# Attention with keys on partitions and transposed channel mixing, in a fused attention and MLP-mixer kernel

## The chip, the cores and the metric

The kernel runs on one core of a Trainium2 chip. The metric is the time of one execution on the device, in microseconds (us). The profile is that of one execution; its span runs from the first to the last instruction.

## What is computed

All numbers are float32, except that the four weights come as float64 words, which the kernel converts. Eight batch elements, 12 heads, 448 tokens, head size 64. The output of attention, heads side by side, goes through a mixer that first mixes tokens and then channels.

```
rmsnorm(x, g) = x / sqrt(mean(x*x) + 1e-6) * g           # over the head size
scores = (rmsnorm(q, g_q) @ rmsnorm(k, g_k).T) / 8
attn   = exp(scores - max(scores)); attn /= sum(attn) + 1e-9
x      = (attn @ v), heads beside one another            # (8, 448, 768)
u      = x + (relu(x.T @ w_tok1) @ w_tok2).T             # 448 -> 256 -> 448
out    = u + relu(u @ w_ch1) @ w_ch2                     # 768 -> 1536 -> 768
```

## The kernel before

Tokens are cut into four chunks of 112 (token 4p + c is row p of chunk c). Attention goes by pairs of heads (48 pairs, six to a batch element) and, within a pair, by four steps, one for each chunk of queries; a step does both heads, called a = 0 and 1.

Before its steps a pair's q and k are loaded (`load_pair`, on SyncE's queue), squared on GpSimd (L208), summed on VectorE (L209), raised to the power -0.5 on GpSimd (L213) and scaled there into `qs` (L218). `trans_qk` transposes them on TensorE (L231), so that the two heads' 64 features lie on 128 partitions, and VectorE copies them out with the gains (L234).

A step's `score` (L247) has the queries stationary and the keys moving. The two heads use the upper and the lower 64 rows of the TensorE array. Scores come out with queries on partitions, 112 x 448, so the row maximum is a reduction on VectorE (L252), and the exponential on ScalarE (L254) takes it as its bias and sums each row on the way. A step later `trans_e` turns the exponentials round in four transposes for each head (L265), which VectorE and ScalarE copy out (L268, L270). Another step later `av` multiplies them with the values, eight products of 64 moving columns (L279). `finish_pair` divides by the sums and writes x with tokens on partitions (L295).

The mixer of one batch element is cut in small pieces. `tok1` (L330) and `tok2` (L340) mix tokens, L343 adds to x; `trans_u` (L350) turns u round, channels on partitions; `ch1` (L365) gives 12 blocks of 128 hidden channels; `ch2` (L380) takes h2 stationary and w_ch2 moving in 384 columns, L385 adds u, and each chunk of 112 tokens is stored.

Weights come in 80 chunks of at most 256 columns. A chunk's words are loaded on ScalarE's queue and converted by five operations on VectorE (L166, L167, L172, L174, L176), two on GpSimd (L169, L170) and one on ScalarE (L171). The first 44 chunks hold the token weights and w_ch1, the last 36 w_ch2.

`merge` interleaves two lists of pieces in proportion to their costs. The attention of batch element b is merged with the mixer of b - 1, that of 0 with the first 44 weight chunks; the last 36 are merged into the first part of the first mixer. The merged order is a priority; within it a scheduler may let an engine's ready instruction go ahead, TensorE's too. The eight PSUM banks are split: three for scores, two for all transposes of attention, one for its output, two for the mixer.

Of the kernel before, what the change touches and what calls it, by code (L numbers as in the profile page):

```python
# [8 lines left out]
F32 = mybir.dt.float32  # L9
U32 = mybir.dt.uint32  # L10
I64 = mybir.dt.int64
# [5 lines left out]

def merge(*lists):
    """Lists of (cost, function), each in its order, interleaved in proportion to their costs."""
# [16 lines left out]
def kernel(  # L36
    ctx: ExitStack,
    tc: tile.TileContext,
    q: bass.AP,
    k: bass.AP,  # L40
    v: bass.AP,
    g_q: bass.AP,
    g_k: bass.AP,
    moe_w_tok1: bass.AP,
    moe_w_tok2: bass.AP,
    moe_w_ch1: bass.AP,
    moe_w_ch2: bass.AP,
    out: bass.AP,
):
    nc = tc.nc  # L50

# [6 lines left out]
    R = S // NS  # tokens of a chunk; token NS * p + c is row p of chunk c  # L58
# [6 lines left out]
    assert S % NS == 0 and R <= P and 2 * D == P and H % 2 == 0  # L65
# [7 lines left out]
    qk_pool = pool("qk_pool", 3)  # L73
    v_pool = pool("v_pool", 4)
    sq_pool = pool("sq_pool", 1)
    qs_pool = pool("qs_pool", 2)
    st_pool = pool("st_pool", 4)
    qkT_pool = pool("qkT_pool", 2)
    e_pool = pool("e_pool", 3)
    eT_pool = pool("eT_pool", 2)  # L80
    x_pool = pool("x_pool", 2)
    ho_pool = pool("ho_pool", 3)
    uT_pool = pool("uT_pool", 1)
# [8 lines left out]
    one_c = const.tile([P, 1], F32, name="one_c")  # L92
# [14 lines left out]
    st = {}  # L107

# [4 lines left out]
    def weight_chunks():  # L113
        """(rows, source, destination, chunks that the destination splits the columns into, or None)."""
# [36 lines left out]
    def weight_convert(i):  # L151
        """Float64 words to the nearest float32: |w| = (1 + high / 2^20 + low / 2^52) * 2^e."""
# [15 lines left out]
        # Exponents past float32's become those of 0 and of infinity.  # L168
        nc.gpsimd.tensor_scalar(ef, e, 1151.0 * 2**20, 896.0 * 2**20, ALU.min, ALU.max)  # L169
        nc.gpsimd.tensor_scalar(e, ef, -896.0 * 2**20, 8.0, ALU.add, ALU.mult)  # L170
        nc.scalar.activation(out=mf, in_=m, func=AF.Identity, bias=one_c[0:rows], scale=2.0**-20)  # L171
# [16 lines left out]

    def load_pair(p):
        b, j = divmod(p, NPAIR)  # L190
        hs = slice(2 * j, 2 * j + 2)
# [4 lines left out]
        vt = v_pool.tile([P, 2, NS * D], F32, name="vt")  # L196
        nc.sync.dma_start(out=vt[0:R], in_=v[b, hs].rearrange("h (p c) d -> p h (c d)", c=NS))
        st["qk", p], st["v", p] = qk, vt

    def norm_pair(p):  # L200
# [4 lines left out]
        for i in range(2):  # L205
            x = qk[0:R, i].rearrange("p h x -> p (h x)")
            sq = sq_pool.tile([P, n * D], F32, name="sq")
            nc.gpsimd.tensor_tensor(out=sq[0:R], in0=x, in1=x, op=ALU.mult)  # L208
            nc.vector.tensor_reduce(  # L209
                out=ms[0:R, i * n:(i + 1) * n], in_=sq[0:R].rearrange("p (n d) -> p n d", d=D),  # L210
# [4 lines left out]
        for i in range(2):  # L215
            qs = qs_pool.tile([P, NS, 2, D], F32, name="qs")
            r = rs[0:R, i * n:(i + 1) * n].rearrange("p (h c) -> p h c", h=2)
            nc.gpsimd.tensor_tensor(  # L218
                out=qs[0:R].rearrange("p c h d -> p h c d"),
                in0=qk[0:R, i].rearrange("p h (c d) -> p h c d", d=D),  # L220
                in1=r.unsqueeze(3).to_broadcast([R, 2, NS, D]), op=ALU.mult)
            st["qs", p, i] = qs
        st.pop(("qk", p))

    def trans_qk(p, i):
# [3 lines left out]
        ps = ps_T.tile([P, 512], F32, name="t_ps", tag="T")  # L229
        for c in range(NS):  # L230
# [3 lines left out]
        nc.vector.tensor_scalar(  # L234
            st["qkT", p][:, i, :], ps[:, 0:S], g_t[:, i:i + 1], None, ALU.mult)

    def score(s):
        p, c = divmod(s, NS)
        qkT = st["qkT", p]
        if c == 0:  # L240
            st["den", p] = st_pool.tile([P, NS, 2], F32, name="den")
        e = e_pool.tile([P, 2, S], F32, name="e")
        nmax = st_pool.tile([P, 2], F32, name="nmax")
        pss = []
        for a in range(2):
            ps = ps_S.tile([P, 512], F32, name="s_ps")
            nc.tensor.matmul(  # L247
                out=ps[0:R, 0:S], lhsT=qkT[a * D:(a + 1) * D, 0, c * R:(c + 1) * R],
                rhs=qkT[a * D:(a + 1) * D, 1, :], start=True, stop=True)
            pss.append(ps)  # L250
        for a in range(2):
            nc.vector.tensor_reduce(  # L252
                out=nmax[0:R, a:a + 1], in_=pss[a][0:R, 0:S], axis=AX_X, op=ALU.max, negate=True)
            nc.scalar.activation(  # L254
                out=e[0:R, a, :], in_=pss[a][0:R, 0:S], func=AF.Exp, bias=nmax[0:R, a:a + 1],
                scale=1.0, accum_out=st["den", p][0:R, c, a:a + 1])
        st["e", s] = e

    def trans_e(s, a):
        e = st["e", s]  # L260
        if a == 0:
            st["eT", s] = eT_pool.tile([P, 2, S], F32, name="eT")
        ps = ps_T.tile([P, 512], F32, name="t_ps", tag="T")
        for kc in range(NS):
            nc.tensor.transpose(  # L265
                ps[0:R, kc * R:(kc + 1) * R], e[0:R, a, kc * R:(kc + 1) * R], ident[0:R, 0:R])
        if a == 0:
# [194 lines left out]
```

## Time and profile before

| | us |
|---|---|
| median of 3 runs | 1982.87 |
| lowest and highest run | 1979.45, 1983.07 |
| span of the profiled execution | 1979.2 |
| median less that span | 3.7 |
| mixer groups of a batch element begin at (L330) | 467.64, 696.57, 925.25, 1154.04, 1383.09, 1611.70, 1833.97 |

The profile gives no time of its execution other than the span. Engines are TensorE (PE; PEld is its loading of the stationary operand), VectorE (DVE), ScalarE (ACT), GpSimd (POOL) and SyncE (SP). A row of the table of groups gives line, engine, operation, output and inputs, shapes and count, then the busy time in us and the mean of one in ns, then the engine's idle time just before and what ended it. A TensorE record's end is modelled, so the cost of one in a dense stretch is read from the start of one group to the start of the next. A float32 product stands there as two records, a transpose as one.

### The profile page before, as it was taken

What the parts mean: (1) busy time and instruction counts of PE and PEld (TensorE: products, weight loads), DVE (VectorE), ACT (ScalarE), POOL (GpSimd) and SP (SyncE); (2) the same over time, 40 slices, a digit from 0 to 9 for tenths busy, and PEclk for the clock granted to TensorE, in tenths of its full rate; (3) what the DMA queues carried; (4) which work ended last, traced back from release to release, by engine and by line L of the source; (5) the groups of instructions that cost most, each with busy time, mean ns of one, the idle gap of its engine ahead of it and who ended that gap; (6) DMA issues with size and microseconds to landing.
All of it is one profiled execution on the core that took longest, in us unless ns stands there. A gap on an engine that the chain in (4) does not pass through costs nothing.

```text
span 1979.2 us, 22557 instructions
## 1 busy us (share of the span) xinstructions
PE 1904.1 (96%) x9152; PEld 1176.1 (59%) x9152; DVE 732.9 (37%) x1513; ACT 477.9 (24%) x1193; POOL 427.9 (22%) x408
## 2 busy tenths in 40 slices
PE   5888888999999999999999999999999999999999
PEld 3556554666656665666656666666666666566554
DVE  5677777233323332332422343233322333222100
ACT  2333333212221222222222122212222122221100
POOL 4444566112211211211121121122112111000000
PEclk9776988999999999999999999999999999999999
DMA  4222232011000100010000110011000100000000
GB/s 118 76 79 86 79 97 78 15 35 31 15 19 22 38 26 14 24 33 28 23 17 25 29 31 19 15 36 36 15 23 16 33 28 15 5 8 14 8 0 28
DMA packets 50535, 66.20 MB, mean 33 GB/s; under 512 B 4416, under 2 KB 36928, under 8 KB 50432
## 3 DMA queue, kind: packets, MB, share of 16 engines
q1 hardware_dynamic: 38656, 44.05, 7.6%
q10 hardware_dynamic: 11776, 20.72, 3.7%
q8 instruction: 72, 1.18, 0.3%
q14 instruction: 31, 0.25, 0.0%
HBM read 53.74 MB, written 11.01 MB: 33 GB/s over the span
## 4 chain that ended last, share of the span: by engine, by line
PE 87%; POOL 5%; DVE 5%; DMA 1%; issue 1%; ACT 0%; ACTq 0%; POOLq 0%; DVEq 0%
PE m_ps L380 26%; PE m_ps L365 21%; PE o_ps L279 14%; PE s_ps L247 9%; PE t_ps L265 7%; PE m_ps L330 4%; PE m_ps L340 3%; PE t_ps L231 2%; POOL rs L213 2%; POOL qs L218 1%; PE m_ps L350 1%; POOL e_t L170 1%; POOL e_t L169 1%; DVE nmax L252 1%; DMA qk<-in_q_dram 1%
## 5 line engine op out<-in xcount | busy, mean ns | idle before, releaser
L380 PE MATMUL m_ps<-wc_sb,h 128*112 128x384 f32 x1536 | 535.2, 491 | 0.0
L365 PE MATMUL m_ps<-uT,wc_sb 128*128 128x448 f32 x1152 | 477.8, 552 | 0.1
L279 PEld LDWEIGHTS o_ps<-vt,eT 112*112 112x112 f32 x3072 | 367.2, 189 | 133.4 <-issue 64.0
L279 PE MATMUL o_ps<-vt,eT 112*112 112x64 f32 x3072 | 369.9, 272 | 15.7 <-DVE eT L268 15.4
L380 PEld LDWEIGHTS m_ps<-wc_sb,h 128*112 128x112 f32 x1536 | 256.1, 177 | 198.0 <-issue 31.6
L254 ACT ACTIVATE e<-s_ps,nmax 112x448 f32<-112x448 f32 x384 | 240.3, 630 | 498.6 <-DVE nmax L252 497.0
L252 DVE TENSOR_REDUCE nmax<-s_ps 112x1 f32<-112x448 f32 x384 | 224.5, 619 | 271.0 <-PE s_ps L247 271.0
L218 POOL TENSOR_TENSOR qs<-qk,rs 112x512 f32<-112x512 f32 x96 | 99.3, 1050 | 999.3 <-PE t_ps L231 998.2
L365 PEld LDWEIGHTS m_ps<-uT,wc_sb 128*128 128x128 f32 x1152 | 205.9, 191 | 182.9 <-issue 180.8
L270 ACT COPY eT<-t_ps 112x448 f32<-112x448 f32 x192 | 102.0, 531 | 595.5 <-PE t_ps L265 585.0
L268 DVE COPY eT<-t_ps 112x448 f32<-112x448 f32 x192 | 119.2, 621 | 338.8 <-PE t_ps L265 179.1
L247 PE MATMUL s_ps<-qkT 64*112 64x448 f32 x768 | 226.1, 614 | 9.2 <-ACT e L254 5.7
L265 PE MATMUL t_ps<-ident,e 112*112 112x112 f32 x1536 | 198.6, 270 | 2.6 <-DVE eT L268 2.6
L265 PEld LDWEIGHTS t_ps<-ident,e 112*112 112x112 f32 x1536 | 169.1, 143 | 52.1 <-issue 33.3
L213 POOL TENSOR_TENSOR rs<-ms,mhalf_c 112x16 f32<-112x16 f32 x48 | 142.4, 2967 | 37.6 <-DVE ms L212 36.6
L208 POOL TENSOR_TENSOR sq<-qk 112x512 f32<-112x512 f32 x96 | 106.5, 1109 | 160.0 <-DMA qk<-in_q_dram 109.1
L247 PEld LDWEIGHTS s_ps<-qkT 64*112 64x112 f32 x768 | 61.7, 180 | 99.0 <-issue 49.1
L385 DVE TENSOR_TENSOR ob<-x,m_ps 112x384 f32<-112x384 f32 x64 | 35.3, 552 | 218.9 <-PE m_ps L380 218.9
L209 DVE TENSOR_REDUCE ms<-sq 112x8 f32<-112x512 f32 x96 | 65.6, 683 | 110.7 <-POOL sq L208 110.7
L340 PE MATMUL m_ps<-h,w_sb 128*112 128x384 f32 x256 | 93.4, 494 | 3.4 <-DVE x L343 3.4
L330 PE MATMUL m_ps<-x,w_sb 112*128 112x384 f32 x256 | 92.4, 505 | 3.9 <-DVE x L295 3.9
L234 DVE TENSOR_SCALAR qkT<-t_ps,g_t 128x448 f32<-128x448 f32 x96 | 63.0, 680 | 85.1 <-PE t_ps L231 85.0
(35 smaller groups left out, 787.1 us busy)
## 6 DMA issues: line engine op xcount, KB each, us to landing
raw<-in_moe_w_ch_dram ACTq DMA_DIRECT2D x72, 256.0 KB, 2.7
qk<-in_q_dram SPq DMA_DIRECT2D x48, 224.0 KB, 3.0
qk<-in_k_dram SPq DMA_DIRECT2D x48, 224.0 KB, 3.2
vt<-in_v_dram SPq DMA_DIRECT2D x48, 224.0 KB, 2.6
out_dram<-ob SPq DMA_DIRECT2D x32, 336.0 KB, 2.7
raw<-in_moe_w_tok_dram ACTq DMA_DIRECT2D x4, 224.0 KB, 5.0
raw<-in_moe_w_tok_dram ACTq DMA_DIRECT2D x2, 256.0 KB, 3.4
raw<-in_moe_w_tok_dram ACTq DMA_DIRECT2D x2, 192.0 KB, 2.4
```

Source lines behind the costliest of these rows:

```text
L213: nc.gpsimd.tensor_tensor(out=rs[0:R], in0=ms[0:R], in1=mhalf_c[0:R].to_broadcast([R, 2 * n]), op=ALU.pow)
L218: nc.gpsimd.tensor_tensor(out=qs[0:R].rearrange("p c h d -> p h c d"), in0=qk[0:R, i].rearrange("p h (c d) -> p h c d", d=D), in1=r.unsque ...
L247: nc.tensor.matmul(out=ps[0:R, 0:S], lhsT=qkT[a * D:(a + 1) * D, 0, c * R:(c + 1) * R], rhs=qkT[a * D:(a + 1) * D, 1, :], start=True, stop ...
L252: nc.vector.tensor_reduce(out=nmax[0:R, a:a + 1], in_=pss[a][0:R, 0:S], axis=AX_X, op=ALU.max, negate=True)
L254: nc.scalar.activation(out=e[0:R, a, :], in_=pss[a][0:R, 0:S], func=AF.Exp, bias=nmax[0:R, a:a + 1], scale=1.0, accum_out=st["den", p][0:R ...
L265: nc.tensor.transpose(ps[0:R, kc * R:(kc + 1) * R], e[0:R, a, kc * R:(kc + 1) * R], ident[0:R, 0:R])
L268: nc.vector.tensor_copy(out=st["eT", s][0:R, a, :], in_=ps[0:R, 0:S])
L279: nc.tensor.matmul(out=o[0:R, c, a, :], lhsT=eT[0:R, a, kc * R:(kc + 1) * R], rhs=vt[0:R, a, kc * D:(kc + 1) * D], start=(kc == 0), stop=( ...
L330: nc.tensor.matmul(out=ps[:, 0:HC], lhsT=w1_sb[0:R, c, jc * P:(jc + 1) * P], rhs=x[0:R, c, cs], start=(c == 0), stop=(c == NS - 1))
L340: nc.tensor.matmul(out=ps[0:R, 0:HC], lhsT=w2_sb[:, jc, c, :], rhs=st["h1", jc][:, cs], start=(jc == 0), stop=(jc == NJ - 1))
L365: nc.tensor.matmul(out=ps[:, 0:S], lhsT=wc1_sb[:, cc, f * P:(f + 1) * P], rhs=st["uT"][:, cc, :], start=(cc == 0), stop=(cc == NC - 1))
L380: nc.tensor.matmul(out=ps[0:R, 0:HC], lhsT=st["h2"][:, f, c * R:(c + 1) * R], rhs=wc2_sb[:, f, cs], start=(f == 0), stop=(f == NF - 1))
```

## The change

**Scores** come out with keys on partitions: `score` has the keys stationary and the queries moving (L251), one half of a pair (two chunks of keys, both heads) at a time. The exponential (L256) has no bias and no sum. There is no row maximum: a gate at the start computes the largest (g_q g_k)^2, and an `If` runs this arm where the scores cannot pass 60 in size; another arm of the same length, with the row maximum, stands behind it.

**Values** are stationary: `av` (L305) multiplies 64 value columns with 448 moving exponentials, the two heads in the left and the right 64 columns of the array, four products for each half pair, straight into channels on partitions. No transposes of e are left.

**Sums** of the exponentials over the key chunks are taken on VectorE in three additions of 112 x 896 (L291, L295), and over partitions by a product with ones (L319); a reciprocal (L328) and a product (L329) follow. The result is uT, channels on partitions.

**Mixing** keeps that form. `trans_x` (L375) makes x for `tok1`; `tok2` (L398) adds to uT; `ch1` (L413) is as before; `ch2` (L425) has w_ch2 stationary and h2 moving, 448 columns; `trans_y` (L437) turns the result round, and two stores of half a batch element each follow (L444).

**Order and space.** TensorE runs in the order in which the code is written; the other engines are still scheduled. Attention of the first two batch elements, and one pair more, goes ahead with the first 44 weight chunks; then the mixer of b is merged with the attention of b + 2, and the last two mixers run alone. q and k have two buffers instead of three, the squares lie in the buffers of `qs`; x and y share one buffer. Four banks hold scores, two the output of attention, two everything else.

```diff
+    ctx.enter_context(tc.manual_schedule(engines={nc.tensor.engine}))
...
-    qk_pool = pool("qk_pool", 3)
+    qk_pool = pool("qk_pool", 2)
...
+    uT_pool = pool("uT_pool", 3)
+    x_pool = pool("x_pool", 1)
...
-    ps_S = pool("ps_S", 3, space=PSUM)
-    ps_T = pool("ps_T", 2, space=PSUM)
-    ps_O = pool("ps_O", 1, space=PSUM)
+    ps_S = pool("ps_S", 4, space=PSUM)
+    ps_O = pool("ps_O", 2, space=PSUM)
     ps_M = pool("ps_M", 2, space=PSUM)
...
-            sq = sq_pool.tile([P, n * D], F32, name="sq")
-            nc.gpsimd.tensor_tensor(out=sq[0:R], in0=x, in1=x, op=ALU.mult)
+            qs = qs_pool.tile([P, NS, 2, D], F32, name="qs")
+            sq = qs[0:R].rearrange("p c h d -> p (c h d)")
+            nc.gpsimd.tensor_tensor(out=sq, in0=x, in1=x, op=ALU.mult)
...
+    def score(p, h):
...
+        for i in range(HN):
+            kc = h * HN + i
...
+                nc.tensor.matmul(
+                    out=ps[0:R, 0:S], lhsT=qkT[a * D:(a + 1) * D, 1, kc * R:(kc + 1) * R],
+                    rhs=qkT[a * D:(a + 1) * D, 0, :], start=True, stop=True)
...
+                nc.scalar.activation(out=e[0:R, a, i, :], in_=pss[a][0:R, 0:S], func=AF.Exp)
...
+    def av(p, h):
...
+                nc.tensor.matmul(
+                    out=o[a * D:(a + 1) * D, 0:S], lhsT=vt[0:R, a, kc * D:(kc + 1) * D],
+                    rhs=e[0:R, a, i, :], start=(kc == 0), stop=(kc == NS - 1))
...
+    def denominator(p):
...
+            nc.tensor.matmul(
+                out=ps[a * D:(a + 1) * D, 0:S], lhsT=one_c[0:R, :], rhs=es[0:R, a, :],
+                start=True, stop=True)
...
+            nc.vector.reciprocal(out=rd[:], in_=ps[:, 0:S])
+        nc.vector.tensor_tensor(out=st["uT", b][:, j, :], in0=st.pop(("o", p))[:, 0:S], in1=rd[:], op=ALU.mult)
...
+    def trans_x(b, j):
...
+            st["x"] = x_pool.tile([P, NS, C], F32, name="x", tag="x")
...
+    def trans_y(b, cc):
...
+            st["y"] = x_pool.tile([P, NS, C], F32, name="y", tag="x")
...
+    for _, fn in merge(att_items(0, AHEAD * per + 2), weight_items(0, len(first))):
+        fn()
     for b in range(B):
...
+        lo = (b + AHEAD) * per + 2
+        att = att_items(lo, lo + per) if b + AHEAD < B else []
+        for _, fn in merge(att, early + late):
...
+    nc.vector.tensor_scalar(small[:], most[:], SCORE_BOUND**2 / D, None, ALU.is_le)
+    with tc.If(nc.values_load(small[0:1, 0:1], min_val=0, max_val=1,
+                              skip_runtime_bounds_check_because="a comparison's result") > 0) as arm:
+        whole(tc, False, *args)
+    with arm.Else():
+        whole(tc, True, *args)
```

TensorE in the middle of channel mixing beside attention, first before, then in the change (a row is a line, an operation, its output and inputs, and how often it stands there in turn; o_ps is the output of attention, s_ps scores, t_ps and m_ps transposes and mixing):

```order
L365 MATMUL m_ps<-uT,wc_sb 128x448 x3
L265 MATMUL t_ps<-ident,e 112x112 x8
L365 MATMUL m_ps<-uT,wc_sb 128x448 x3
L247 MATMUL s_ps<-qkT 112x448 x2
L279 MATMUL o_ps<-vt,eT 112x64 x4
L365 MATMUL m_ps<-uT,wc_sb 128x448 x3
L279 MATMUL o_ps<-vt,eT 112x64 x4
L265 MATMUL t_ps<-ident,e 112x112 x8
```
```order
L251 MATMUL s_ps<-qkT 112x448 x4
L305 MATMUL o_ps<-e,vt 64x448 x4
L413 MATMUL m_ps<-uT,wc_sb 128x448 x12
L251 MATMUL s_ps<-qkT 112x448 x4
L319 MATMUL m_ps<-es,one_c 64x448 x2
L305 MATMUL o_ps<-e,vt 64x448 x4
L413 MATMUL m_ps<-uT,wc_sb 128x448 x9
L233 MATMUL m_ps<-ident,qs 128x112 x8
```
The transposes of e are gone; scores stand in fours, and the values of the half pair before follow them at once. The q and k transposes (L233) stand in the mixer's banks, here in the middle of a block of six L413 products.

TensorE in the opening, after the first transposes, in the change:

```order
L251 MATMUL s_ps<-qkT 112x448 x8
L305 MATMUL o_ps<-e,vt 64x448 x4
L233 MATMUL m_ps<-ident,qs 128x112 x8
L251 MATMUL s_ps<-qkT 112x448 x4
L305 MATMUL o_ps<-e,vt 64x448 x4
L251 MATMUL s_ps<-qkT 112x448 x4
L319 MATMUL m_ps<-es,one_c 64x448 x2
L305 MATMUL o_ps<-e,vt 64x448 x4
L233 MATMUL m_ps<-ident,qs 128x112 x8
```
This goes on to the thirteenth pair with nothing of the mixer between; before, the mixer's first product stood there after six pairs.

ScalarE where the mixer of one batch element ends and the next begins, in the change, with what each row waits for (DMAHW are transfers):

```order
L439 COPY y<-m_ps 112x4x128 [waits PE_49]
L240 ACTIVATE qkT<-m_ps,g_t 128x448 [waits PE_49]
L439 COPY y<-m_ps 112x4x128 [waits PE_49]
L380 COPY x<-m_ps 112x4x128 [waits DMAHW6_49,DMAHW7_49,PE_49,Activation_49]
L380 COPY x<-m_ps 112x4x128 [waits PE_49] x2
L393 ACTIVATE h_2909<-m_ps 128x384 [waits PE_49]
```
The first copy of x now waits for the two transfers that empty y; before, x had buffers of its own.

More of the change, by code (lines that the diff above doesn't have):

```diff
@@ L35, with whole @@
 @with_exitstack
[L36 to L49, printed above, removed]
+def whole(ctx, tc, shifted, q, k, v, g_q, g_k, moe_w_tok1, moe_w_tok2, moe_w_ch1, moe_w_ch2, out):
     nc = tc.nc
+    ctx.enter_context(tc.manual_schedule(engines={nc.tensor.engine}))
     B, H, S, D = q.shape
@@ L259, in trans_e @@
[L259 to L267, printed above, removed]
-            nc.vector.tensor_copy(out=st["eT", s][0:R, a, :], in_=ps[0:R, 0:S])
-        else:
-            nc.scalar.copy(out=st["eT", s][0:R, a, :], in_=ps[0:R, 0:S])
-            st.pop(("e", s))
@@ new lines, in trans_x @@
+    def trans_x(b, j):
+        if j == 0:
+            st["x"] = x_pool.tile([P, NS, C], F32, name="x", tag="x")
+        ps = m_tile()
+        for c in range(NS):
+            nc.tensor.transpose(
+                ps[0:R, c * P:(c + 1) * P], st["uT", b][:, j, c * R:(c + 1) * R], ident[:, :])
+        src = ps[0:R, :].rearrange("p (c n) -> p c n", c=NS)
+        dst = st["x"][0:R, :, j * P:(j + 1) * P]
+        if j % 2:
+            nc.scalar.copy(out=dst, in_=src)
+        else:
+            nc.vector.tensor_copy(out=dst, in_=src)
```

333 lines of the change are left out of this document (192 added, 141 removed).

## The prediction

> **What bounds the kernel now.** The page's busy shares and clock row come first, then a table of stages.
>
> ```profile
> PE 1904.1 (96%) x9152; PEld 1176.1 (59%) x9152; DVE 732.9 (37%) x1513; ACT 477.9 (24%) x1193; POOL 427.9 (22%) x408
> PEclk9776988999999999999999999999999999999999
> ```
> ```profile
> 23.00:119.20 96.20, 82.70 (x386) 57.22 (x386) 65.91 (x165) 34.42 (x88) 40.92 (x54) 0.84 0.27 76
> 119.20:165.00 45.80, 38.78 (x180) 28.17 (x181) 30.83 (x79) 15.89 (x41) 22.29 (x30) 0.65 0.28 80
> 265.00:315.00 50.00, 40.89 (x180) 24.38 (x179) 39.07 (x99) 15.21 (x35) 38.72 (x41) 0.90 0.34 94
> 365.00:415.00 50.00, 50.00 (x246) 30.72 (x244) 15.81 (x29) 9.90 (x26) 12.02 (x8) 1.00 0.10 30
> 467.64:696.57 228.93, 228.14 (x1145) 140.78 (x1145) 75.42 (x139) 55.01 (x139) 42.12 (x30) 1.00 0.09 25
> ```
> The columns are PE, PEld, DVE, ACT, POOL busy, granted clock, DMA share, GB/s. In a steady batch (six of them, 467.64 to 1833.97) TensorE works 228.14 of 228.93 us at full clock, VectorE 75: only TensorE's work counts. Before about 365 us VectorE is busy up to 39.07 of 50 us with weight conversion, TensorE waits and its clock falls to 0.65. So: price TensorE's steady work, then the opening apart. The timeline of TensorE in a steady batch, and the last chain:
>
> ```profile
> 1000.66 2.43 PE L365 MATMUL m_ps<-uT,wc_sb 128*128 128x448 f32 x6
> 1002.93 0.55 PE L265 MATMUL t_ps<-ident,e 112*112 112x112 f32 x4
> 1003.41 1.01 PE L247 MATMUL s_ps<-qkT 64*112 64x448 f32 x4
> 1004.35 2.52 PE L365 MATMUL m_ps<-uT,wc_sb 128*128 128x448 f32 x6
> 1006.71 1.70 PE L279 MATMUL o_ps<-vt,eT 112*112 112x64 f32 x16
> 1008.24 2.47 PE L365 MATMUL m_ps<-uT,wc_sb 128*128 128x448 f32 x6
> 1010.55 0.93 PE L265 MATMUL t_ps<-ident,e 112*112 112x112 f32 x8
> 1011.32 2.43 PE L365 MATMUL m_ps<-uT,wc_sb 128*128 128x448 f32 x6
> ```
> ```profile
> 1833.97 10.38 PE m_ps L330 x32
> 1844.35 10.34 PE m_ps L340 x32
> 1858.49 54.39 PE m_ps L365 x144
> 1912.88 61.93 PE m_ps L380 x192
> ```
> A product is two records. From start to start: a 448-column record 54.39/144 = 0.378 us, a product 0.756; a transpose 0.77/8 = 0.096; eight attention-value products 1.53, 0.096 a record where 64 of 448 columns would be 0.054: they wait for their weights; two scores on the two row halves 0.94, not 4 x 0.378 = 1.51, so they overlap, at 0.19 over the 0.756 of one, and 0.09 more on what follows (2.36 against 2.27). A batch of before is then 24 x 1.03 scores, 24 x 1.53 values, 192 + 48 + 24 transposes at 0.096, 10.4 + 10.3 + 54.4 + 61.9 mixing = 223.8 us; the trace has 228.9, a factor of 1.02 that I keep.
>
> **The change, steady part.** Removed per batch: 18.4 us of transposes of e, 36.7 of value products with 64 moving columns, 61.9 of 384-column products. Added: per half pair two score couples (4 x 0.378 + 0.19 = 1.70), two couples of value products on column halves, per pair one couple with ones, and 24 + 24 transposes of 128 columns (0.11 each, 2.6 + 2.6).
>
> Column couples have no row in before. If they overlap as row couples do, a half's values cost 1.70 and the sums 0.76; if not, 8 x 0.378 = 3.02 and 1.51. I take the overlap, by the nearest row, L247. A pair is then 3.4 + 3.4 + 0.76 + 0.77 (eight transposes) + 0.2 after mode changes = 8.5 us, six 51.2. Mixing: 10.4, tokens second 12 x 0.756 = 9.1, 54.4, channel second 72 x 0.756 = 54.4, 5.2 of transposes: 133.5. Sum 184.7 x 1.02 = 188.4.
>
> Three new waits lie on TensorE, which now runs in written order with nothing to pull ahead:
>
> ```profile
> L234 DVE TENSOR_SCALAR qkT<-t_ps,g_t 128x448 f32<-128x448 f32 x96 | 63.0, 680 | 85.1 <-PE t_ps L231 85.0
> 1855.32 3.06 PE L350 MATMUL m_ps<-ident,x 112*128 112x112 f32 x20 [0.26 <-DVE x L343]
> qk<-in_q_dram SPq DMA_DIRECT2D x48, 224.0 KB, 3.0
> out_dram<-ob SPq DMA_DIRECT2D x32, 336.0 KB, 2.7
> 303.64 3.25 PE L279 MATMUL o_ps<-vt,eT 112*112 112x64 f32 x16 [5.02 <-DVE eT L268]
> 306.69 4.01 PE L365 MATMUL m_ps<-uT,wc_sb 128*128 128x448 f32 x6
> 310.53 0.93 PE L265 MATMUL t_ps<-ident,e 112*112 112x112 f32 x8
> ```
> First, q and k transposes lost their own two banks; through the two mixing banks the second waits for one eviction, 0.68 and signals, 1 us a pair, 6 a batch (0 to 12). Second, x goes back to tokens in 24 transposes with no other work between: uncovered ones cost 0.153 (3.06/20), so 1.4 more. Third, x and y share one buffer: x of the next batch cannot be copied until y has left. Copy of y 0.6, transfer of half a batch (672 KB, between 2.7 and twice that: 4.1), copy of x 0.65, signals 0.4, less 0.9 of transposes that fit the free banks: 4.8 idle. Queued behind it are 16 transposes and all of the mixing; ScalarE's and VectorE's later exponentials and sums stand behind the waiting copies too. After a 5.02 us wait at 303.64 the next two groups took 3.05 + 3.84 us where 1.53 + 2.31 is usual, so 3 us more: 7.8 a batch (bounds 2 to 11). A batch: 188.4 + 6 + 1.4 + 7.8 = 203.6, against 228.9.
>
> Without the row maximum (L252) and the accumulated sums nothing moves: TensorE did not wait for them in the steady part. Added VectorE work: by the rows below 8.1 us a pair, six pairs 49 and three copies and twelve additions of about 0.65 for mixing, 58 a batch against 75 before, hidden under 188 of TensorE; GpSimd keeps its 42. If that cover went, the cost is the opening's. Loads of q and k have two buffers instead of three: one is free again when GpSimd has scaled the pair before the last, a pair's time ahead of its need, and a load takes 3.0, so I cost it at nothing; SyncE's two larger stores a batch instead of four stand behind loads that wait for products already done.
>
> **The opening.** Twelve and a half pairs now run with 44 of the 80 weight chunks and no mixing.
>
> ```profile
> 19.37 2.01 PE L231 MATMUL t_ps<-ident,qs 112*128 112x112 f32 x8 [19.37 <-POOL qs L218]
> L100 DVE TENSOR_SCALAR g_t<-g_t 128x1 f32<-128x1 f32 x1 | 0.2, 154 | 4.9 <-DMA g_t<-in_g_q_dram 4.9
> L176 DVE TENSOR_TENSOR wc_sb<-m_t,e_t 128x256 f32<-128x256 f32 x72 | 31.6, 439 | 0.0
> L295 DVE TENSOR_TENSOR x<-o_ps,rd 112x512 f32<-112x512 f32 x48 | 33.1, 690 | 87.5 <-PE o_ps L279 87.5
> L294 DVE RECIPROCAL rd<-rd 112x8 f32<-112x8 f32 x48 | 9.6, 201 | 1.3
> L293 DVE TENSOR_SCALAR rd<-den 112x8 f32<-112x8 f32 x48 | 8.4, 174 | 34.1 <-ACT e L254 34.1
> L209 DVE TENSOR_REDUCE ms<-sq 112x8 f32<-112x512 f32 x96 | 65.6, 683 | 110.7 <-POOL sq L208 110.7
> L166 DVE TENSOR_SCALAR e_t<-raw 128x256 uint32<-128x256 uint32 x74 | 22.9, 310 | 0.1
> L167 DVE TENSOR_SCALAR m_t<-raw 128x256 uint32<-128x256 uint32 x74 | 25.4, 343 | 0.0
> L172 DVE SCALAR_TENSOR_TENSOR m_t<-raw,m_t 128x256 f32<-128x256 uint32 x74 | 36.5, 494 | 0.1
> L174 DVE SCALAR_TENSOR_TENSOR e_t<-raw,e_t 128x256 uint32<-128x256 uint32 x74 | 31.3, 423 | 43.0 <-POOL e_t L170 43.0
> L208 POOL TENSOR_TENSOR sq<-qk 112x512 f32<-112x512 f32 x96 | 106.5, 1109 | 160.0 <-DMA qk<-in_q_dram 109.1 <-DVE ms L209 44.8 <-DVE rd L293 5.2
> L218 POOL TENSOR_TENSOR qs<-qk,rs 112x512 f32<-112x512 f32 x96 | 99.3, 1050 | 999.3 <-PE t_ps L231 998.2
> L213 POOL TENSOR_TENSOR rs<-ms,mhalf_c 112x16 f32<-112x16 f32 x48 | 142.4, 2967 | 37.6 <-DVE ms L212 36.6
> ```
> The gate on g waits 4.9 us for its load, four short VectorE operations 0.7, and loading and branching on five engines, which no row shows (0 to 5; I take 3.4): 9. First transposes at 19.4 + 9 = 28.4.
>
> VectorE per pair: three sums of 896 elements; 256 take 0.439 and 512 take 0.690, so about 1.07 each, 3.2; a 448-element reciprocal, 0.68 if it goes as L234, up to 2.8 if all that L294 has over L100 (47 ns for 8 elements) is per element; by L294 over L293, 3.4 ns an element, 2.2, which I take; the product 0.63, one qkT 0.68, two squares' sums 1.37: 8.1. A chunk takes 0.310 + 0.343 + 0.494 + 0.423 + 0.439 = 2.0, 3.5 chunks a pair 7.1. Sum 15.2 a pair if VectorE never waits; at 39.07 of 50, its fullest stage in before, 19.4. TensorE's 8.5 would be 17 at half clock. The squares now lie in the buffers of the scaled q and k, so the chain squares, sums, power, scaling starts only after the last pair's transposes; 2.2 + 1.4 + 3.0 + 2.1 and signals, about 9, and with what is queued between its steps still under 17. I take 17 a pair: 212 us, ending near 240. The first mixed batch still has 36 chunks, 72 us of VectorE beside 8.1 x 4 and 6 of mixing, 110 in the part up to the end of channel first (76.5 of mixing and four pairs), where TensorE has 111: 20 us of waits (0 to 45).
>
> Sum: 28.4 + 212 + (203.6 + 20) + 5 x 203.6 + batch six alone (133.5 x 1.02 + 1.4 + 7.8 = 145.4) + batch seven with its last transfer (143.4) = 1771 us, against a span of 1979.2. The median of the runs shown lies 3.7 above the span; I add the same: 1775.
>
> **Rivals.** *Column couples run one after the other.* For it: both halves use the same rows, and no row of before shows columns split. Against: L247's halves start together. It adds 1.32 a half and 0.76 a pair, 3.4: 125 us over 36 pairs and about 45 in the opening: 1945. Chance 0.12.
>
> *Column records also wait for their weights (slower).* In before a 64-column record takes 1.53/16 = 0.096, its weights'; were that added to each of a pair's 20 column records in turn, 0.474 each, a pair costs 5.3 more, and by the same scale (50 us for each us a pair) about 265: 2040. It turns slower than before at 4.1 a pair, 0.415 us a record. Against: L365's 144 records reload the same rows every 0.378 with the load hidden. Chance 0.05. The Trainium skill, "TensorE: Matmul & The Clock Gate", section "The mechanism" of Part 3, says weight loads overlap running matmuls only where the row groups differ, which would be this rival; L365 speaks against the rule. The same page's "Measured speedup vs the span model" has 2.38 times for three column tiles; no run here shows one.
>
> *The opening is cheap*: VectorE without waits and a short reciprocal, 13.7 a pair (41 less), no first-batch waits (20), transfers mostly hidden (25): 1690. Chance 0.08. *The opening is dear*: 19.4 a pair (30 more), 25 more in the first batch, upper bounds of the bank waits (30): 1860. Chance 0.08.
>
> That the second arm runs is excluded: in the reference's inputs the largest product of g_q and g_k is 5.26, and the bound on it is 60/8 = 7.5.
>
> **Numbers.** Forecast 1775, chance 0.67. The range 1690 to 1885 leaves out the two column rivals and little else. About 0.2% is what a measurement here can tell: faster 0.94 (the forecast, both openings and most of the serial case), same 0.01, slower 0.05.
>
> **What would show it.** Steady batches of about 204 us; L305 half pairs at 1.7 us start to start (3.0: serial; over 3.3: slower); first L375 near 245 us; a wait of about 5 us before an L375 group in each batch, ended by the copy of x, with a colder clock behind it; RECIPROCAL near 2.2 us. A steady batch above 215, or an opening beyond 300 us, makes the prediction wrong.

## The result, and the profile after

The changed kernel takes 1813.39 us (median of 4 runs, 1812.42 to 1814.12) against 1981.16 (4 runs, 1978.88 to 1983.07) for the kernel before on the same chip: a ratio of 0.9165, with the 95% interval [0.9144, 0.9186]. It is faster by 168 us, where 206 were forecast; 1813 lies inside the range. The profiled execution has a span of 1811.9 us.

The busy shares, and the granted clock in 40 slices of 45 us:

```profile
PE 1570.2 (87%) x5248; PEld 743.7 (41%) x5248; DVE 627.2 (35%) x957; ACT 355.1 (20%) x713; POOL 446.8 (25%) x408
PEclk8776778989999999999999999999999999999999
```
TensorE's records fell from 9152 to 5248 and its busy time by 334 us, twice what the span lost. The rest went into the opening: it fills the first seven slices, some 300 us, and TensorE's clock is granted at 0.6 to 0.8 of full speed there.

The table of stages, with the same columns as before the prediction (PE, PEld, DVE, ACT, POOL, granted clock, DMA share, GB/s): two windows of the opening, the first mixed batch, and a steady one. The last two are cut at the first transposes of x (L375) of successive batch elements.

```profile
80.00:130.00 50.00, 28.19 (x108) 10.91 (x108) 34.21 (x64) 14.76 (x31) 28.98 (x27) 0.71 0.22 68
130.00:180.00 50.00, 29.00 (x116) 10.49 (x112) 29.69 (x57) 12.15 (x26) 28.11 (x29) 0.73 0.24 75
290.20:518.50 228.30, 199.41 (x658) 93.37 (x656) 121.20 (x241) 54.85 (x112) 82.31 (x97) 0.95 0.20 58
518.50:719.00 200.50, 190.40 (x657) 90.39 (x656) 63.11 (x69) 39.63 (x79) 42.09 (x31) 0.98 0.09 28
```
This steady batch takes 200.5 us instead of 228.9, a little under the 203.6 of the prediction, and TensorE fills 190.4 of it. In the opening nobody is full: VectorE, which should have been the bound there, works 29.69 to 34.21 of 50 us, GpSimd 28 to 29, TensorE 28 to 29. The opening ends at 290.2 instead of about 240. Engines that wait for each other in turn would look like this.

TensorE's timeline in a steady batch (start, length, line, tiles, shape, records):

```profile
608.12 1.76 PE L251 MATMUL s_ps<-qkT 64*112 64x448 f32 x8
609.82 0.97 PE L319 MATMUL m_ps<-es,one_c 112*64 112x448 f32 x4
610.62 1.67 PE L305 MATMUL o_ps<-e,vt 112*64 112x448 f32 x8
612.22 2.15 PE L413 MATMUL m_ps<-uT,wc_sb 128*128 128x448 f32 x5
```
From start to start, scores take 1.70, the couple with ones 0.80, half a pair's values 1.60: both heads' eight records of 0.378 in the time of four. The column couples overlap.

The end of one batch element and the begin of the next, and the stores' row of the DMA issues (transfers, KB of each, median us to landing):

```profile
718.36 0.65 PE L437 MATMUL m_ps<-ident,uT 128*112 128x128 f32 x4
719.03 1.30 PE L375 MATMUL m_ps<-ident,uT 128*112 128x128 f32 x8
724.74 3.84 PE L375 MATMUL m_ps<-ident,uT 128*112 128x128 f32 x16 [4.41 <-ACT x L380]
728.51 3.65 PE L390 MATMUL m_ps<-x,w_sb 112*128 112x384 f32 x8
```
```profile
out_dram<-y SPq DMA_DIRECT2D x16, 672.0 KB, 4.3
```
Eight transposes of x fit into the two free banks, then TensorE stands for 4.41 us until the copy L380 may write the buffer that y leaves. The next 16 transposes take 3.8 us where 2.6 would follow from the first eight's 1.3: the granted clock is 0.50 in these 3.8 us and 0.76 in the 3.5 us after them, against 1.00 in the eight before the wait. That is the cold tail of the prediction.

Now the opening. VectorE's and GpSimd's rows beside TensorE's, in one pair, in order of time; the brackets give the idle time before a row and what ended it:

```profile
148.82 4.16 POOL L217 TENSOR_TENSOR rs<-ms,mhalf_c 112x16 f32<-112x16 f32 x1 [1.21 <-DVE ms L216]
...
153.06 2.04 POOL L221 TENSOR_TENSOR qs<-qk,rs 112x512 f32<-112x512 f32 x2
...
155.19 0.88 POOL L165 TENSOR_SCALAR e_t<-e_t 128x256 f32<-128x256 uint32 x2
...
156.14 1.13 POOL L166 TENSOR_SCALAR e_t<-e_t 128x256 uint32<-128x256 f32 x2
...
156.58 0.43 DVE L170 SCALAR_TENSOR_TENSOR e_t<-raw,e_t 128x256 uint32<-128x256 uint32 x1 [6.37 <-POOL e_t L166]
...
157.65 1.09 DVE L291 TENSOR_TENSOR es<-e 112x896 f32<-112x896 f32 x1
...
162.60 2.95 DVE L328 RECIPROCAL rd<-m_ps 128x448 f32<-128x448 f32 x1
...
165.70 0.98 PE L233 MATMUL m_ps<-ident,qs 112*128 112x112 f32 x4 [7.48 <-DVE rd L328]
...
166.76 1.04 POOL L211 TENSOR_TENSOR qs<-qk 112x512 f32<-112x512 f32 x1 [3.18 <-PE m_ps L233]
...
169.30 3.82 POOL L217 TENSOR_TENSOR rs<-ms,mhalf_c 112x16 f32<-112x16 f32 x1 [1.50 <-DVE ms L216]
```
GpSimd does the power (4.16 us) and the scaling (2.04) of a pair, and two small conversion steps of the weights, L165 and L166, stand behind these in its order. VectorE has handed its chunk over and waits 6.37 us for them, in order, with the sums of the exponentials (L291) and the reciprocal (L328) queued behind. TensorE needs one of the two mixing banks for the second transposes of q and k, and that bank is held until the reciprocal has read the sums: 7.48 us of standing. Only when those transposes have read the scaled k can GpSimd write the next squares into its buffer (L211); VectorE then sums them, and GpSimd begins its next power at 169.30, 20.5 us after the last one. The chain that ended last, followed back through the opening (31 to 290 us), runs over the same rows: GpSimd's power has 18.8% of it, its scaling 9.8, its two conversion steps 8.4 and 8.1, its squares 2.8, VectorE's reciprocal 13.4, and no row of TensorE more than 2.5. TensorE's cold clock is therefore not the pace here.

The waits of the opening (25 to 290 us; engine, tile and line, what it waited for, us in total, times, longest):

```profile
PE m_ps L233 <- DVE rd L328: 105.2, 12, 11.5
DVE e_t L170 <- POOL e_t L166: 88.8, 36, 6.4
```

### The profile page after: what moved, and what is told of

Its sections match the earlier page's. It is cut to its first block, busy times and chain, and to the rows that moved or that the text cites. A ratio compares the mean times of both kernels' runs of the same rounds, so it can differ in the third digit from the quotient of the medians.

```text
span 1811.9 us, 13526 instructions
## 1 busy us (share of the span) xinstructions
PE 1570.2 (87%) x5248; PEld 743.7 (41%) x5248; DVE 627.2 (35%) x957; ACT 355.1 (20%) x713; POOL 446.8 (25%) x408
## 4 chain that ended last, share of the span: by engine, by line
PE 70%; DVE 13%; POOL 10%; DMA 2%; issue 2%; ACT 2%; ACTq 0%; DVEq 0%; POOLq 0%
PE m_ps L425 24%; PE m_ps L413 22%; PE s_ps L251 6%; PE o_ps L305 5%; PE m_ps L390 4%; DVE rd L328 4%; POOL rs L217 4%; PE m_ps L398 3%; DVE es L295 2%; POOL e_t L166 2%; POOL qs L221 2%; POOL e_t L165 2%; DMA out_dram<-y 2%; PE m_ps L375 2%; PE m_ps L233 1%
## 5 line engine op out<-in xcount | busy, mean ns | idle before, releaser
L413 PE MATMUL m_ps<-uT,wc_sb 128*128 128x448 f32 x1152 | 452.0, 547 | 13.3 <-ACT h L417 6.3
L425 PE MATMUL m_ps<-h,wc_sb 128*128 128x448 f32 x1152 | 450.4, 544 | 9.2 <-DVE uT L430 5.8
L413 PEld LDWEIGHTS m_ps<-uT,wc_sb 128*128 128x128 f32 x1152 | 215.9, 191 | 236.5 <-issue 209.6
L211 POOL TENSOR_TENSOR qs<-qk 112x512 f32<-112x512 f32 x96 | 102.4, 1068 | 830.4 <-PE m_ps L233 769.9
L425 PEld LDWEIGHTS m_ps<-h,wc_sb 128*128 128x128 f32 x1152 | 213.4, 190 | 220.3 <-issue 204.0
L256 ACT ACTIVATE e<-s_ps 112x448 f32<-112x448 f32 x384 | 180.9, 546 | 313.5 <-PE s_ps L251 211.1
L251 PE MATMUL s_ps<-qkT 64*112 64x448 f32 x768 | 191.3, 613 | 16.5 <-DVE qkT L238 6.5
L295 DVE TENSOR_TENSOR es<-es,e 112x896 f32<-112x896 f32 x96 | 108.1, 1126 | 213.8 <-ACT e L256 210.3
L233 PE MATMUL m_ps<-ident,qs 112*128 112x112 f32 x384 | 60.8, 287 | 138.2 <-DVE rd L328 105.2
L305 PE MATMUL o_ps<-e,vt 112*64 112x448 f32 x768 | 171.9, 571 | 0.0
L328 DVE RECIPROCAL rd<-m_ps 128x448 f32<-128x448 f32 x48 | 141.6, 2951 | 5.8 <-PE m_ps L319 5.8
L233 PEld LDWEIGHTS m_ps<-ident,qs 112*128 112x128 f32 x384 | 46.3, 154 | 175.1 <-issue 138.6
L291 DVE TENSOR_TENSOR es<-e 112x896 f32<-112x896 f32 x48 | 52.7, 1099 | 187.3 <-ACT e L256 187.3
L251 PEld LDWEIGHTS s_ps<-qkT 64*112 64x112 f32 x768 | 67.8, 188 | 120.0 <-issue 89.6
L305 PEld LDWEIGHTS o_ps<-e,vt 112*64 112x64 f32 x768 | 53.0, 143 | 111.4 <-issue 111.4
L398 PE MATMUL m_ps<-w_sb,h 128*128 128x448 f32 x192 | 80.1, 559 | 13.7 <-DVE rd L328 11.1
```

What stands on the lines that cost most here:

```text
L233: nc.tensor.transpose(ps[:, c * R:(c + 1) * R], qs[0:R, c].rearrange("p h d -> p (h d)"), ident[0:R, 0:R])
L251: nc.tensor.matmul(out=ps[0:R, 0:S], lhsT=qkT[a * D:(a + 1) * D, 1, kc * R:(kc + 1) * R], rhs=qkT[a * D:(a + 1) * D, 0, :], start=True, st ...
L256: nc.scalar.activation(out=e[0:R, a, i, :], in_=pss[a][0:R, 0:S], func=AF.Exp)
L295: nc.vector.tensor_tensor(out=es[0:R], in0=es[0:R], in1=e[0:R, :, i, :], op=ALU.add)
L305: nc.tensor.matmul(out=o[a * D:(a + 1) * D, 0:S], lhsT=vt[0:R, a, kc * D:(kc + 1) * D], rhs=e[0:R, a, i, :], start=(kc == 0), stop=(kc == ...
L328: nc.vector.reciprocal(out=rd[:], in_=ps[:, 0:S])
```

## The experiments

What sets the pace of the opening was the open question, and the overlap of the columns and the price of the y buffer were to be shown by themselves. For the opening, theory A takes VectorE's own work as the pace, with the reciprocal of 2.95 us in it. Theory C says that VectorE and GpSimd take turns: their work alternates because each stands in order behind the other's result. Between them lies theory B, holds by ScalarE's queue or by a bank, which the first two runs try. "Opening" below is the start of the first L375, 290.2 in the change; a single run is meant unless a range is given. The kernel before took 1980.06 beside the runs on loads, banks, reciprocal and head order, 1974.93 (median of 8, 1971.49 to 1983.47) beside the last three, and 1983.42 beside the other four; so a few us between runs of different groups say little.

**Weight loads on SyncE's queue instead of ScalarE's.**

```diff
-            nc.scalar.dma_start(
+            nc.sync.dma_start(
```


> The weight chunks' loads are issued on SyncE's queue instead of ScalarE's; no other edit, and VectorE's work is the same. Theory A (VectorE's own work sets the opening's pace, 21.3 us a pair): no change, first L375 at 290 +/- 6 us. Theory B (queues in order hold one another up: a load that waits on ScalarE for its raw buffer holds the exponentials, they the sums, the reciprocal, the bank, the transposes): 2 to 5 us less a pair, first L375 at 225 to 265, span 1750 to 1785. Steady batches stay at 201 in both.

1816.7 us, opening 294.7, a steady batch 201. The opening did not get shorter: the loads in ScalarE's queue are not the pace. VectorE's waits for GpSimd fell from 88.8 to 67.2 us all the same, so their sum alone doesn't measure the loop.

**A third mixing bank, one less for scores.**

```diff
-    ps_S = pool("ps_S", 4, space=PSUM)
+    ps_S = pool("ps_S", 3, space=PSUM)
-    ps_M = pool("ps_M", 2, space=PSUM)
+    ps_M = pool("ps_M", 3, space=PSUM)
```


> One PSUM bank goes from the scores (four to three) to the mixing banks (two to three). Theory A: no change in the opening, 290 +/- 6. Theory B, with the bank that the reciprocal holds as the link that counts: the 105 us of L233 waiting for the reciprocal go, the opening gets 30 to 90 us shorter. Steady batches: 3 to 8 us less, if the transposes' and evictions' waits there are the bank's too; a loss of a score bank may cost 0 to 4.

1810.67 us, opening 291.8, steady 201.4. The longest wait of the opening, 105.2 us of TensorE for the reciprocal, is gone, and the opening is as long as it was; the steady batch doesn't gain the 3 to 8 us expected either. The waits of the opening (25 to 290 us):

```profile
DVE e_t L170 <- POOL e_t L166: 85.6, 34, 6.4
PE s_ps L251 <- DVE qkT L238: 56.5, 9, 11.7
PE s_ps L251 <- ACT e L256: 31.9, 9, 5.9
```
TensorE now stands at the scores instead, for VectorE's copies and for ScalarE's exponentials, while VectorE's wait for GpSimd is what it was. The bank is a link in the loop and does not set its length.

**A copy in place of the reciprocal.**

```diff
-            nc.vector.reciprocal(out=rd[:], in_=ps[:, 0:S])
+            nc.vector.tensor_copy(out=rd[:], in_=ps[:, 0:S])
```


> The reciprocal of the sums is replaced by a copy of them, so the division is left out and the output is not the reference's. 2.95 us become about 0.7 in each pair. Theory A: the opening loses just that, 12.5 x 2.3 = 28 us, first L375 near 262. Theory B: the bank comes free earlier too, up to twice that, 230 to 260. Steady batches: 0 to 4 us less.

1768.11 us, opening 269.0, steady 198.4, first mixed batch 220.2. The group of L328 in the change, and in this kernel (busy us and mean ns of one):

```profile
L328 DVE RECIPROCAL rd<-m_ps 128x448 f32<-128x448 f32 x48 | 141.6, 2951 | 5.8 <-PE m_ps L319 5.8
```
```profile
L328 DVE COPY rd<-m_ps 128x448 f32<-128x448 f32 x48 | 29.6, 617 | 5.8 <-PE m_ps L319 5.8
```
Taking 2.33 us off each pair shortens the opening by 21 of a possible 12.5 x 2.33 = 29, less than either theory expected. The reciprocal lies in the loop, but VectorE's wait for GpSimd stays at 85.0 us, and 20 us a pair remain. Theory A is not excluded by this run, since a bound by VectorE would also give way.

**The conversion's two GpSimd steps on VectorE.**

```diff
-        nc.gpsimd.tensor_scalar(ef, e, 1151.0 * 2**20, 896.0 * 2**20, ALU.min, ALU.max)
-        nc.gpsimd.tensor_scalar(e, ef, -896.0 * 2**20, 8.0, ALU.add, ALU.mult)
+        nc.vector.tensor_scalar(ef, e, 1151.0 * 2**20, 896.0 * 2**20, ALU.min, ALU.max)
+        nc.vector.tensor_scalar(e, ef, -896.0 * 2**20, 8.0, ALU.add, ALU.mult)
```


> The two conversion steps of a weight chunk that GpSimd did (L165, L166) go to VectorE. Theory A (VectorE's own work sets the opening's pace): 44 chunks x 2 x about 0.35 = 31 us more work, first L375 at 310 to 330. Theory C (VectorE and GpSimd take turns: VectorE's L170 waits 6.4 us in its order for conversion steps that stand on GpSimd behind the power and the scaling, and the sums and the reciprocal stand behind L170): the wait goes and 2.5 us a pair are added, first L375 at 225 to 265. Steady batches unchanged, 201.

1744.23 us, opening 226.7, first mixed batch 221.2, steady 201.1. This is the decisive run: VectorE is given more work, 0.6 us a chunk, and the opening becomes 63.5 us shorter. The same windows as above:

```profile
80.00:130.00 50.00, 35.01 (x142) 13.21 (x144) 45.66 (x97) 17.85 (x38) 38.21 (x16) 0.80 0.32 94
130.00:180.00 50.00, 34.98 (x148) 13.02 (x148) 48.48 (x99) 19.35 (x41) 40.96 (x18) 0.86 0.36 100
```
VectorE is busy 45.66 and 48.48 of 50 us, and the wait for GpSimd's steps no longer exists. First transposes start at 22.8 here, so a pair takes (226.7 - 22.8)/12.5 = 16.3 us. Theory A, by which more work on VectorE lengthens the opening, falls for the change as it stands; it holds for this kernel, in which VectorE is at last the bound. GpSimd's busy time rises too, although it has two steps less a chunk: its scaling takes longer. The group in the change, then in this kernel:

```profile
L221 POOL TENSOR_TENSOR qs<-qk,rs 112x512 f32<-112x512 f32 x96 | 98.4, 1046 | 3.8
```
```profile
L221 POOL TENSOR_TENSOR qs<-qk,rs 112x512 f32<-112x512 f32 x96 | 131.4, 1389 | 3.8
```
In the opening alone it is 1.02 us in the change and 2.05 here. VectorE was busy 172 of 265 us there and 191 of 202 here; what lengthens the scaling was not tried by itself.

**One batch element ahead instead of two.**

```diff
-    AHEAD = 2
+    AHEAD = 1
```


> Attention runs one batch element ahead of the mixer instead of two, so the opening has six and a half pairs, not twelve and a half, with the same 44 chunks. Theory that an opening pair costs what it costs because nothing else is there to fill it (22 to 28 us a pair with 6.8 chunks each): first L375 at 165 to 205, seven mixed batches, span 1750 to 1795. Rival: the opening is bound by the chunks, 44 x 4 us or more, and the next batch gets what is left: first L375 above 220, span 1800 to 1830.

1782.89 us, opening 193.0, first mixed batch 236.9, steady 201, all as the first theory had it. The opening is 97.2 us shorter, the first mixed batch 8.6 longer, and batch six, which now has attention beside it, some 58 longer (201 instead of 143): being two ahead costs 31 us here. The opening still needs all 44 chunks and has half the pairs to put beside them.

**One ahead, and y in a buffer of its own.**

```diff
-    uT_pool = pool("uT_pool", 3)
+    uT_pool = pool("uT_pool", 2)
+    y_pool = pool("y_pool", 1)
...
-            st["y"] = x_pool.tile([P, NS, C], F32, name="y", tag="x")
+            st["y"] = y_pool.tile([P, NS, HC], F32, name="y")
...
-    AHEAD = 2
+    AHEAD = 1
```


> As the run with attention one ahead, and y has a buffer of its own of half a batch element instead of sharing that of x. If the store of y is what TensorE waits for at the seven ends of a batch, each loses its 4.4 us of idle and about 3 of colder clock: a steady batch 193 to 195 instead of 201, the span 40 to 55 us below that run. If the copies of x are late for another reason, or y's halves now wait for each other, 0 to 20.

1743.75 us, opening 193.6, steady 195.3. Against the kernel with one ahead and the shared buffer, 39 us less, just short of the 40 to 55 expected: 5.7 a steady batch. TensorE's waits for the copy of x fall from 4.41 us a batch to 0.9 (3.4 in four batches).

**Both heads on the same columns.**

```diff
-                    out=o[a * D:(a + 1) * D, 0:S], lhsT=vt[0:R, a, kc * D:(kc + 1) * D],
-                    rhs=e[0:R, a, i, :], start=(kc == 0), stop=(kc == NS - 1))
+                    out=o[h * D:(h + 1) * D, 0:S], lhsT=vt[0:R, a, kc * D:(kc + 1) * D],
+                    rhs=e[0:R, a, i, :], start=(i == 0 and a == 0), stop=(i == HN - 1 and a == 1))
```


> All four value products of a half pair go to the same 64 columns (the first half of the keys left, the second right), so that none can run beside its neighbour; heads are summed together, so the output is not the reference's. If columns overlap in the change, a half takes near 3.0 us instead of 1.6 to 1.7: a steady batch 12 x 1.35 = 16 us longer, 215 to 219; the opening, which TensorE does not pace, 0 to 10 longer; span 1905 to 1935.

1885.21 us, a steady batch 217.3 to 218.2, 16.7 longer. Half a pair's values, and what follows, in TensorE's timeline:

```profile
609.01 3.17 PE L305 MATMUL o_ps<-e,vt 112*64 112x448 f32 x8
612.12 1.40 PE L413 MATMUL m_ps<-uT,wc_sb 128*128 128x448 f32 x3
```
3.11 us from start to start against 1.60: the column split is worth 1.51 a half, twelve times a batch, 18.1, of which 16.7 came through. The expectation missed in the opening, and so in the span: it ended at 267.5, 22.7 us sooner and not up to 10 later, although TensorE had more to do. VectorE's rows stand in another order there, its waits for GpSimd are 55.8 us instead of 88.8, and TensorE's clock is 0.80 to 0.90 instead of 0.71 to 0.76; which of these shortened it was not tried, so only the steady part is compared.

**Heads one after the other in the code.**

```diff
-        for i in range(HN):
-            kc = h * HN + i
-            for a in range(2):
+        for a in range(2):
+            for i in range(HN):
+                kc = h * HN + i
```


> The four value products of a half pair are ordered head by head (left, left, right, right columns) instead of in couples. If couples overlap because neighbours use different columns, the half takes near 3.0 us instead of 1.7 in the steady part, less where the middle two still overlap (2.6): a steady batch 12 x 0.9 to 1.3 = 11 to 16 us longer, 212 to 217. If the array works so on any order, no change.

1815.54 us, opening 292.0, steady 201.1. The values of half a pair and what follows:

```profile
598.73 1.73 PE L305 MATMUL o_ps<-e,vt 112*64 112x448 f32 x8
600.39 1.02 PE L413 MATMUL m_ps<-uT,wc_sb 128*128 128x448 f32 x2
```
1.66 us: the heads overlap even when the code has one after the other. The trace doesn't tell whether a step of compilation or the chip put them beside each other.

**Both mends together: conversion on VectorE, y in small tiles.** Two ahead as in the change; y goes out in six stores of 224 KB a batch element, through tiles that share the two buffers of h1.

```diff
+        nc.vector.tensor_scalar(ef, e, 1151.0 * 2**20, 896.0 * 2**20, ALU.min, ALU.max)
...
-            st["y"] = x_pool.tile([P, NS, C], F32, name="y", tag="x")
+        y = h1_pool.tile([P, NS, P], F32, name="y", tag="ho")
```


> Attention two ahead as in the change; the two GpSimd conversion steps on VectorE, and y in tiles of 128 channels that take turns in the two buffers of h1, six stores a batch of 224 KB, instead of y in the buffer of x. If the two costs found are separate (GpSimd's place in VectorE's order in the opening, the store of y at a batch's end), the gains add: first L375 at 222 to 232, steady batches 194 to 196, span 1742 less 7 x 5.7 = 1700 to 1710. If h1 now waits for the last stores, or the shorter runs of the stores are slow enough to be waited for, 1715 to 1745.

1700.79 us (median of 4 runs, 1699.87 to 1702.01), a ratio to the kernel before of 0.8617 [0.8603, 0.8631]; opening 223.8, first mixed batch 220.9, steady 195.3. It beats both kernels. The busy tenths of VectorE in 40 slices, the stores, and the boundary of two batch elements on TensorE:

```profile
DVE  6999998832242234233333224323332322001000
...
out_dram<-y SPq DMA_DIRECT2D x48, 224.0 KB, 2.8
```
```profile
1225.98 1.40 PE L375 MATMUL m_ps<-ident,uT 128*112 128x128 f32 x8
1227.81 1.08 PE L375 MATMUL m_ps<-ident,uT 128*112 128x128 f32 x8 [0.42 <-DVE x L382]
1230.67 2.85 PE L390 MATMUL m_ps<-x,w_sb 112*128 112x384 f32 x8 [0.35 <-DVE x L382]
```
VectorE is full from the second slice to the sixth, and the 4.41 us before the transposes have become 0.42. The two gains found apart, 69.2 and 39.1, are 108 of the 112.6 us by which it beats the change: they add, as expected.

**Every other chunk's two steps on VectorE**, y in small tiles.

```diff
+        eng = nc.vector if i % 2 else nc.gpsimd
+        eng.tensor_scalar(ef, e, 1151.0 * 2**20, 896.0 * 2**20, ALU.min, ALU.max)
+        eng.tensor_scalar(e, ef, -896.0 * 2**20, 8.0, ALU.add, ALU.mult)
```


> As the run before it, but only every other chunk's two steps go to VectorE. If VectorE, now nearly always busy in the opening, is the bound with all of them on it, half of them saves up to 15 us there, provided the chunks left on GpSimd aren't waited for: first L375 at 210 to 225. If VectorE stops at the first chunk that GpSimd has not done, it lies between the two: 230 to 265.

1759.28 us, opening 282.5, steady 195.3. The expectation missed: half of the steps bring 8 us, not half of 63. Fewer waits, but nearly as long ones (25 to 282.5 us):

```profile
DVE e_t L171 <- POOL e_t L167: 65.3, 18, 5.9
```
VectorE still stops, in order, at the first chunk that lies with GpSimd behind a power. The two chunks or so a pair that stay on GpSimd are enough to make the two take turns. This also speaks against GpSimd simply having had too much work: the two steps have 16.5% of the change's chain between 31 and 290 us, 43 us, and half of that, 21, would then have been saved.

**The same half, one ahead, y in its own buffer.** The edits of the kernel one ahead with its own y, and the split by `i % 2`.

> One batch element ahead, y with its own buffer, every other chunk's two steps on VectorE. Against the run with y's own buffer (span 1742, first L375 at 193.6, first mixed batch 237): VectorE's work to the end of the opening rises from 146 to 162 us of 171; if GpSimd's turn was the wait there too, the opening gets 0 to 20 us shorter and the first mixed batch 0 to 15; if VectorE is full, 0 to 15 longer.

1747.81 us, opening 198.8, steady 195.3: an opening 5 us longer than with all steps on GpSimd. VectorE's waits for GpSimd were 38.8 us without the split and 43.5 with it. VectorE isn't full (138 of 199 us), so neither branch of the expectation gives the reason; that GpSimd has fewer powers in its order for each chunk here, 44 chunks beside six and a half pairs, is a guess.

## Why the prediction was right, and where it was off

**The columns** (right). Half a pair's values were put at 1.70 if the couples overlap and 3.02 if not; 1.60 and, on the same columns, 3.11 were measured. Both the choice and its rival were priced well. The rival in which column records wait for their weights is out: by its 0.474 a record, half a pair's eight would take 3.79. Records of L425 don't wait either: 24 take 9.30 us (the row is shown below), 0.39 each, little more than L365's 0.378. The Trainium skill, "TensorE: Matmul & The Clock Gate", section "The mechanism" of Part 3, has in its list that weight loads overlap running matmuls only where the row groups differ; L425 and L305 reload the same rows for every record, and their times disagree with that line. The first paragraph of the same section also lets loads into a background weight buffer run ahead, and with that the times agree.

**The steady batch** (right, for somewhat other reasons). 203.6 was forecast, about 200.0 is the mean of five (201.0 of the four with six pairs; the fifth has five). The wait for y was put at 7.8; 4.41 idle and the slower transposes behind it were there, and the kernel with its own y shows the whole at 5.7, so idle (forecast 4.8) was right and the cold tail was put too high. The two mixing banks were put at 6 a batch: in the steady part TensorE's waits at L233 sum to far less,

```profile
PE m_ps L375 <- ACT x L380: 4.4, 1, 4.4
PE m_ps L233 <- DVE qkT L238: 1.7, 2, 0.9
PE m_ps L398 <- DVE rd L328: 1.4, 1, 1.4
```
1.7 us in the batch from 518.5, where only two pairs show one. Those 4.3 and 2.1 less, and some 4 us of small waits that the sum didn't have, make 201 (200.5 in this batch).

**The gate** (over by 7.7). First transposes at 20.7 instead of 28.4. The start, in the timeline:

```profile
2.14 0.21 DVE L520 TENSOR_TENSOR gg<-g 1x64 f32<-1x64 f32 x1 [2.14 <-DMA g<-in_g_k_dram]
...
2.87 0.14 DVE L523 TENSOR_SCALAR small<-most 1x1 int32<-1x1 f32 x1
...
3.68 0.36 SPq L193 DMA_DIRECT2D qk<-in_q_dram  x1
```
The load of g landed at 2.14, not 4.9, and reading the register and branching took 3.68 - 3.01 = 0.67, not 3.4, a figure that stood on no row.

**The opening** (wrong, and the one large miss). 17 us a pair were forecast, 21.6 came: (290.2 - 20.7)/12.5. Over 12.5 pairs that is 57 us, more than the whole difference of 38 between forecast and result. The step that failed is the sentence that the chain squares, sums, power, scaling takes "about 9, and with what is queued between its steps still under 17". It treated VectorE's 15.2 us of work as the pace and GpSimd's queue as cover. But the conversion passes from VectorE to GpSimd and back, so GpSimd's queue doesn't only delay the next pair's q and k: it holds VectorE, with the sums and the reciprocal behind it, and these hold TensorE's bank. Moving the two steps away from GpSimd takes the loop apart (16.3 a pair, near the 17 and its 15.2 when VectorE is full), which shows the cause; the bank (opening 291.8 with a third one) and the loads in ScalarE's queue (294.7 without them) are shown not to set the pace. That 17 and 16.3 lie so close is in part luck: the 17 was meant for a kernel in which the two steps stay on GpSimd.

Two sizes lie in the loop as well. The reciprocal was taken at 2.2, with bounds 0.68 and 2.8, and took 2.95, above the upper one; GpSimd's power, taken at 3.0, takes 3.98 us in the mean of the opening (2.89 in steady batches). The copy in place of the reciprocal says what the first can be worth: 2.33 us less a pair gave 1.8 (its first transposes start at 21.9), so the missing 0.75 accounts for about 7 us of the 57. The power's 1.0 a pair would be up to 12 more; no run tries it.

**First mixed batch and the end** (under by 12.5, over by 3.1). The windows are cut at L375, ahead of the wait for y, while the sum has that wait, 7.8, at the end of the batch before. So the first mixed batch's 228.3 holds no such wait and stands against 223.6 - 7.8 = 215.8; the last batch's 150.5 holds one and stands against 143.4 + 7.8 = 151.2; batch six took 143.0 against 145.4. In the first mixed batch TensorE idles 28.9 us; a steady one idles 10.1, of which 4.4 for y: 23 more, where 20 were forecast. The rest is TensorE's busy time, 199.4 against 190.4, at a granted clock of 0.95 instead of 0.98, which the sum didn't have. In the last batch, with no attention to fill it, the blocks of L425 follow one another like this:

```profile
1793.43 0.63 DVE uT L430
1794.10 9.30 PE m_ps L425 x24
1803.43 0.63 DVE uT L430
```
9.30 us of products, then 0.70 until VectorE has added the block, freed its bank, and the next work begins; TensorE puts four transposes into that gap and idles 0.28. By terms, against a forecast span of 1771: -7.7 gate, +57.5 opening, +12.5 first mixed, -18 five steady batches, -3.1 end: 1812. The last term, 3.7 outside the span, was 1.5. That 1813 came as near to 1775 as it did owes something to luck: the opening's 57.5 were partly offset by the gate and the steady batches.

**What stays open.** Each of these edits also lets the scheduler put VectorE's rows in another order, and what that alone is worth in the opening was not measured. Why VectorE waited 55.8 us with the same columns and 88.8 without was not tried by itself; nor was a kernel in which GpSimd keeps the two steps but has them ahead of the power in its order, the direct test of the order against the place. One ahead with all steps on VectorE was not tried either.

## What to carry to other kernels

Before you call the fullest engine the pace of a stage, follow a chain that passes from one in-order engine to another and back: if the second has a long instruction ahead in its queue, both take turns, and the stage lasts longer than either one's work. Neither engine is then full; giving the first engine more work, so that the chain never leaves it, can shorten the stage, while moving half of it brought little here. A wait that disappears without shortening the stage (the bank here) was a link, not the cause.

## What the runs showed of the hardware

- Float32 products on the left and the right 64 columns overlap although they use the same 112 rows: 1.60 us for eight records, 3.11 on the same columns; and 1.66 when the code has the heads one after the other.
- A reciprocal of 128 x 448 from a bank takes 2.95 us on VectorE, 6.6 ns an element; a copy of the same takes 0.62.
- A branch on a value computed on VectorE delayed the first load by 0.67 us after that value was there.
- The scaling of 112 x 512 on GpSimd takes 1.02 us in the change's opening and 2.05 in that of the kernel with the conversion on VectorE, where VectorE is busy 191 of 202 us; the power takes 2.89 us in steady batches, 3.98 and 4.54 in the two openings. What lengthens them was not tried by itself.
- After TensorE had stood for 4.41 us, its granted clock was 0.50 for the next 3.8 us and 0.76 for the 3.5 us after.
